# A chunked-attention and two-MLP kernel on one core: 64x64 products of scores and x put on four corners of the array instead of two

## The chip, the core and the metric

The kernel runs on one core of a Trainium2 chip. Its engines are TensorE (PE in the rows: matmuls; PEld: the loads of their weights), VectorE (DVE), ScalarE (ACT), GpSimd (POOL) and SyncE (SP), which issues the transfers between HBM and the core. Each engine works off its own list in order and waits for the others by semaphores. Matmul results go to PSUM, eight banks of 2 KB in each of 128 partitions. The metric is the device time of one execution in microseconds.

## The reference

```python
# attention in chunks of 64 tokens: 8 batches, 8 heads, 576 tokens, head dimension 64
scores = 1/8 * q_c @ k_c.T            # 64x64 for each chunk and head
attn = exp(scores - rowmax); attn = attn / (rowsum + 1e-9)
x = attn @ v_c                        # then reshaped to 4608 tokens x 512
# first MLP, 512 -> 1024 -> 512
h = x @ w_in;  sm = softmax(h);  solu = h * sm
x = (layernorm(solu) * g_ln) @ w_out
# second MLP, 512 -> 2048 -> 512
h = x @ w_in2;  g = max(h, 0) + alpha * min(h, 0)
out = g @ w_out2
```

All inputs are float32.

## The kernel before

The 4608 tokens are 36 tiles of 128. In each tile lie two chunks (c) of 64 tokens with 8 heads, and the heads are numbered by three bits (g, w, e in the code). Phase 1 does attention and the first MLP tile by tile and converts the weights of the second MLP beside it; phase 2, from about 520 us on, does the second MLP and is not touched by the change.

Each tile goes through short stages with two-letter names, and the lists FIRST and STEP write out by hand in which order they are emitted; every engine gets its own instructions in that order. FIRST covers the start. STEP then runs thirteen times, for i = 10, 12, ... 34, two tiles a round (the last has one transposed tile left); `qk+3` in it means stage qk of tile i+3. The stages that matter here:

- `qk` (L383 on): the scores, 16 products of 64x64 in float32, q against k, into a tile sc of one PSUM bank; two tiles' scores share the two banks of the pool ps_z, which the tile zt uses at other times.
- `qm` (VectorE): row maximum (nm) and difference (e), read from sc. `qe` (ScalarE): exponential. `qs`, `qn`: row sum and scaling.
- `tr` (TensorE): four 128x128 transposes of the attention into a bank et. `te` (ScalarE): its copy ets to SBUF.
- `pv` (L440 on): 16 products of 64x64, v against ets, into a bank xd. `xh` (ScalarE) and `xl` (VectorE) split xd in a high and a low part.
- `hm`: h = x @ w_in, 24 matmuls of 512 columns into the two banks of the single tile h. `hx` (VectorE, maximum), `he` (ScalarE, exponential) and `so` (VectorE, writes sl) read h; the next `hm` may write h when `so` is done with it.
- `zt`: eight transposes of the normalized sl into tile zt; `zh`, `zl` split it. `ya`, `yb`: the matmuls yps with w_out.
- `conv`: conversion of a block of the second MLP's weights, with hi, pos and neg on ScalarE.

A 64x64 product uses a quarter of the 128x128 array: the half of the rows from which its operands come (partitions 0 to 63 or 64 to 127 of SBUF) and the half of the columns that stand for its output's partitions. I call these quarters corners, (row half, column half). In `qk` and `pv` the operands' partitions and the output's are the same slice r, so that only (0,0) and (1,1) occur, one after the other:

```python
r = slice(64 * e, 64 * e + 64)
nc.tensor.matmul(ps[r, c, g, w], t[r, 0, c, g, w], t[r, 1, c, g, w], start=True, stop=True)
```

The pool ps_a holds two banks with the tags sc and et. In the STEP rounds et and xd of the odd tile use one of them and those of the even tile the other (function `bank`).

Of the kernel before, what the change touches and what calls it, by code (L numbers as in the profile page):

```python
# [45 lines left out]
def order(text):  # L46
# [3 lines left out]

FIRST_TILES = 10
FIRST = order(
    """
# [19 lines left out]
    """  # L73
    tr+1 zh-2 v+4 q+6 hm+0 zl-2 conv+0 tr+2 te+1 hx+0 qk+3 te+2 pv+1 qk+4 qm+3 he+0 qm+4 xh+1 so+0 pv+2
    xl+1 ya-5 qe+3 zt-1 qs+3 conv+0 sq+0 qe+4 qs+4 ye-6 yx-5 xh+2 hm+1 zh-1 zv+0 xl+2 v+3 pw+0 hx+1 yb-5
# [22 lines left out]
def tile_chunk_attention_solu_prelu(  # L98
# [75 lines left out]
    def phase1():  # L174
        with ExitStack() as c1, ExitStack() as c0:
# [14 lines left out]
            yp = R("y", 4)  # L190
            ps_a = L("ps_a", 1, space=PSUM)
            ps_h = L("ps_h", 1, space=PSUM)
            ps_z = R("ps_z", 1, space=PSUM)
            ps_y = R("ps_y", 2, space=PSUM)
# [181 lines left out]

            pair = [None]

            def bank(i):
                return "sc" if i >= FIRST_TILES + 2 and i % 2 == 0 else "et"  # L380

            def qk(i):
                if i < FIRST_TILES + 3:  # L383
                    ps = ps_a.tile([128, 2, 2, 2, CH], F32, name="sc", tag="sc")
                elif i % 2:
                    pair[0] = ps_z.tile([128, 2, 2, 2, 2, CH], F32, name="sc", tag="zt")
                    ps = pair[0][:, 0]
                else:
                    ps = pair[0][:, 1]
                t = qs.pop(i)  # L390
                for c in range(2):
                    for g in range(2):
                        for w in range(2):
                            for e in range(2):
                                r = slice(64 * e, 64 * e + 64)
                                nc.tensor.matmul(  # L396
                                    ps[r, c, g, w], t[r, 0, c, g, w], t[r, 1, c, g, w], start=True, stop=True
                                )
                sc[i] = ps

            def qmax(i):
                ps = sc.pop(i)
                nm = sm.tile([128, H], F32, name="nm", tag="nm", bufs=1)
                psv = ps.rearrange("q c g w k -> q (c g w) k")
                nc.vector.tensor_reduce(out=nm, in_=psv, op=ALU.max, axis=AX.X, negate=True)
                e = at.tile([128, H, CH], F32, name="e", tag="e")
                nc.vector.tensor_tensor(out=e, in0=psv, in1=nm.unsqueeze(2).to_broadcast([128, H, CH]), op=ALU.add)
                ee[i, 0] = e
# [19 lines left out]
            def tr(i):  # L428
                assert i not in rs
                e = ee.pop((i, 1)).rearrange("q (j w) k -> q j (w k)", w=2)  # L430
                ps = ps_a.tile([128, NP, 128], F32, name="et", tag=bank(i))
                for p in range(NP):
                    nc.tensor.transpose(ps[:, p], e[:, p], ident)
                att[i, 0] = ps
# [6 lines left out]
            def pv(i):  # L441
                assert ("v", i) in done
                a = att.pop((i, 1)).rearrange("k (c g e q) -> k c g e q", c=2, g=2, e=2)
                v = vs.pop(i)
                if i < 8:
                    ps = ps_y.tile([128, NP, 2, CH], F32, name="xd", tag="yps")
                else:
                    ps = ps_a.tile([128, NP, 2, CH], F32, name="xd", tag=bank(i))
                for c in range(2):
                    for g in range(2):  # L450
                        for e in range(2):
                            for w in range(2):
                                r = slice(64 * w, 64 * w + 64)
                                nc.tensor.matmul(  # L454
                                    ps[r, 2 * g + e, c], v[r, c, g, e], a[r, c, g, e], start=True, stop=True
                                )
                pvs[i] = ps.rearrange("d p c q -> d p (c q)")

            def xhigh(i):
                if 2 <= i < 6:  # L460
                    t = xt[i // 2 - 1]
                    xh, xl = t[:, i % 2, 0], t[:, i % 2, 1]
                else:
                    xh = xp.tile([128, NP, 128], F32R, name="xh", tag="xh")
                    xl = xp.tile([128, NP, 128], F32R, name="xl", tag="xl")
                nc.scalar.activation(out=xh, in_=pvs[i], func=AF.Copy)
                xs[i, 0] = xh, xl

            def xlow(i):
                xh, xl = xs[i, 1] = xs.pop((i, 0))  # L470
                nc.vector.tensor_tensor(out=xl, in0=pvs.pop(i), in1=xh.bitcast(F32), op=ALU.subtract)

# [181 lines left out]
            for name, i in FIRST:  # L654
                if name in "ho" and i >= UO:
                    run_post(next(u for u in range(len(units)) if ("a", u) not in done) + 1)
                else:
                    emit(name, i)
            twice = TWICE
            k = 0  # L660
# [533 lines left out]
```

## Time and profile before

| | |
|---|---|
| median of three runs | 1255.19 us (1254.41 to 1256.19) |
| the profiled execution, its own time | 1252.65 us |
| its span, first to last instruction | 1250.9 us |
| TensorE busy | 1222.3 us, 98% |
| VectorE, ScalarE, GpSimd busy | 72%, 54%, 26% |
| share of TensorE in the chain that ended last | 88% |

The profile is one execution. Its rows give start and length of instructions in us from the span's start, merged where equal ones follow each other (x32 is 32 of them); brackets at a row's end say how long the engine had been idle before and what ended that. Ends of matmuls are modelled and neighbours overlap in the pipeline, so TensorE's work is measured by distances between starts. PEclk is the granted clock of TensorE, 1.00 for 2.4 GHz and 0.50 for 1.2 GHz.

### The profile page before, as it was taken

The page shows a single profiled execution, that of the slowest core. Times are in us where ns is not written, and L with a number is a line of the kernel's source. Part 1 is how long each engine was busy: PE and PEld are TensorE (multiplying, and loading weights), DVE is VectorE, ACT ScalarE, POOL GpSimd, SP SyncE. Part 2 cuts the span into 40 slices and gives each one's busy share as a digit, 9 for nine tenths or more (in the row PEclk, how much of TensorE's full clock was granted, in tenths as well). Part 3 has the DMA queues.
Part 4 walks back from the last instruction along what each step waited for, and adds up shares of the span by engine and source line. Part 5 has one row for each costly group of instructions (what it writes and reads, how often), then busy time and mean ns, then how long its engine had stood idle before and what let it go on. Part 6 is the DMA issues. An engine that isn't in the chain of part 4 may idle for free.

```text
span 1250.9 us, 20791 instructions
## 1 busy us (share of the span) xinstructions
PE 1222.3 (98%) x7830; PEld 1058.4 (85%) x7830; DVE 898.9 (72%) x1274; ACT 674.7 (54%) x1061; POOL 330.0 (26%) x336
## 2 busy tenths in 40 slices
PE   5889999999999999999999999999999999999998
PEld 4778888888888888888888999988888888889998
DVE  7986676667766766337777777777885967859594
ACT  6684555555655555345666666566543434444442
POOL 3454266445755765323020030300000000000000
PEclk8899999999999999999999999999999999999999
DMA  9534276555755652559653545479983837547463
GB/s 355 185 85 127 84 223 200 159 171 170 236 172 185 207 189 104 188 222 361 225 185 122 169 156 180 148 255 305 334 336 124 297 101 245 176 142 244 140 215 101
DMA packets 148277, 244.64 MB, mean 196 GB/s; under 512 B 14672, under 2 KB 81360, under 8 KB 147664
## 3 DMA queue, kind: packets, MB, share of 16 engines
q1 hardware_dynamic: 145872, 241.22, 56.7%
q10 hardware_dynamic: 2304, 2.10, 0.5%
q8 instruction: 61, 1.00, 0.3%
q14 instruction: 40, 0.33, 0.1%
HBM read 154.93 MB, written 88.34 MB: 194 GB/s over the span
## 4 chain that ended last, share of the span: by engine, by line
PE 88%; DVE 2%; issue 1%; ACT 1%; DVEq 0%
PE h L480 9%; PE ov L1032 8%; PE ox L1032 8%; PE oz L1032 8%; PE hv L789 7%; PE hx L789 7%; PE hz L789 7%; PE yps L170 5%; PE yps L172 5%; PE yps L171 5%; PE h L486 5%; PE oy L1032 4%; PE hy L789 3%; PE zt L546 2%; PE xd L454 2%; PE sc L396 2%
## 5 line engine op out<-in xcount | busy, mean ns | idle before, releaser
L828 DVE SCALAR_TENSOR_TENSOR g<-ng,nal,g 128x512 f32<-128x512 f32 (+1 forms) x160 | 119.6, 747 | 51.2 <-ACT g L701 49.4
L701 ACT ACTIVATE ng<-g 128x512 f32<-128x512 f32 (+1 forms) x120 | 70.8, 590 | 121.9 <-DVE g L695 121.3
L170 PE MATMUL yps<-zz,wo_h 128*128 128x512 f32 x288 | 115.3, 400 | 0.0
L172 PE MATMUL yps<-zz,wo_l 128*128 128x512 f32 x288 | 112.6, 391 | 0.0
L171 PE MATMUL yps<-zz,wo_h 128*128 128x512 f32 x288 | 112.3, 390 | 0.0
L789 PE MATMUL hv<-th,w 128*128 128x512 f32 (+1 forms) x320 | 105.1, 369 | 0.4 <-DVE g L695 0.3
L789 PE MATMUL hz<-th,w 128*128 128x512 f32 (+1 forms) x320 | 104.9, 368 | 0.4 <-DVE g L695 0.2
L789 PE MATMUL hx<-th,w 128*128 128x512 f32 (+1 forms) x320 | 104.7, 368 | 0.2 <-ACT g L701 0.2
L494 DVE TENSOR_REDUCE st<-h 128x1 f32<-128x1024 f32 x36 | 44.1, 1224 | 69.2 <-PE h L486 69.2
L1032 PE MATMUL ov<-rhi,w 128*128 128x512 f32 (+3 forms) x308 | 93.1, 364 | 0.0
L1032 PE MATMUL ox<-rhi,w 128*128 128x512 f32 (+1 forms) x304 | 92.8, 366 | 0.0
L1032 PE MATMUL oz<-rhi,w 128*128 128x512 f32 (+1 forms) x304 | 92.8, 366 | 0.0
L701 ACT ACTIVATE rhi<-rt 128x1024 fp32r<-128x1024 f32 (+1 forms) x56 | 54.1, 970 | 63.2 <-PE ov L1032 18.0
L698 POOL TENSOR_TENSOR yt<-y,y 128x512 f32<-128x512 f32 (+1 forms) x20 | 26.2, 1333 | 219.7 <-DMA y<-yd 219.7
L500 ACT ACTIVATE eh<-h,st 128x1024 f32<-128x1024 f32 x36 | 40.2, 1115 | 70.0 <-DVE st L494 66.8
L698 DVE TENSOR_TENSOR rlo<-rt,rhi 128x1024 fp32r<-128x1024 f32 (+1 forms) x56 | 61.5, 1105 | 15.3 <-ACT rhi L701 14.9
L701 ACT ACTIVATE g<-g 128x512 f32<-128x512 f32 (+1 forms) x120 | 70.4, 586 | 2.6
L480 PE MATMUL h<-wi_h,xh 128*128 128x512 f32 x256 | 71.4, 401 | 0.0
L480 PE MATMUL h<-wi_l,xh 128*128 128x512 f32 x256 | 68.6, 390 | 0.0
L789 PEld LDWEIGHTS hv<-th,w 128*128 128x128 f32 x320 | 59.6, 188 | 9.4 <-DVE g L695 0.9
L789 PEld LDWEIGHTS hz<-th,w 128*128 128x128 f32 x320 | 59.6, 188 | 8.6 <-DVE g L695 1.2
L789 PEld LDWEIGHTS hx<-th,w 128*128 128x128 f32 x320 | 59.6, 188 | 8.1 <-ACT g L701 0.6
(175 smaller groups left out, 3198.2 us busy)
## 6 DMA issues: line engine op xcount, KB each, us to landing
gd<-g SPq DMA_DIRECT2D x96, 256.0 KB, 2.9
qkt<-in_qk SPq DMA_DIRECT2D x36, 512.0 KB, 5.0
w<-wod SPq DMA_DIRECT2D x28, 448.0 KB, 5.0
gd<-g SPq DMA_DIRECT2D x64, 192.0 KB, 1.8
raw<-in_moe_w_out SPq DMA_DIRECT2D x24, 511.8 KB, 4.3
rc<-gd SPq DMA_DIRECT2D x22, 512.0 KB, 4.0
rd<-gd SPq DMA_DIRECT2D x22, 512.0 KB, 4.9
vt<-in_v SPq DMA_DIRECT2D x36, 256.0 KB, 4.3
```

The lines of the kernel that those rows point to most:

```text
L170: nc.tensor.matmul(o, lh, rh, start=first, stop=False)
L171: nc.tensor.matmul(o, lh, rl, start=False, stop=False)
L172: nc.tensor.matmul(o, ll, rh, start=False, stop=last)
L480: nc.tensor.matmul(ps[:, n], xh[:, kk], w[:, kk, 512 * n:512 * n + 512], start=(kk == 0 and w is wi_h), stop=False,)
L486: nc.tensor.matmul(ps[:, n], xl[:, kk], wi_h[:, kk, 512 * n:512 * n + 512], start=False, stop=(kk == K1 - 1),)
L494: nc.vector.tensor_reduce(out=st[:, 0:1], in_=hs[i], op=ALU.max, axis=AX.X, negate=True)
L500: nc.scalar.activation(out=e, in_=hs[i], func=AF.Exp, bias=st[:, 0:1], accum_out=st[:, 1:2])
L698: eng.tensor_tensor(out=out, in0=a, in1=b, op=ALU.subtract)
L701: nc.scalar.activation(out=out, in_=in_, func=func, **k)
L789: nc.tensor.matmul(self.ps[x], w[:, a, i, k], d[:, k], start=(p not in CHAINED and k + j == 0), stop=(k == 1 and j == 2), skip_group_check ...
L828: nc.vector.scalar_tensor_tensor(out=self.g[t], in0=self.n[t], scalar=nal_sb[:, f:f + 1], in1=self.g[t], op0=ALU.mult, op1=ALU.add)
L1032: nc.tensor.matmul(bank[key, m][:, e:f], W[2 * j + k][:, a, i, 128 * m:128 * m + 128], d[:, k, e:f], start=(p not in CHAINED and j + k + q ...
```

## The change

From tile 13 on (QUAD), `qk` and `pv` go through all four corners in the order (0,0), (1,1), (0,1), (1,0), four products at a time. The outputs of products with operands in rows 0 to 63 go to one PSUM bank and those of rows 64 to 127 to another, so each of a tile's sc and xd lies across two banks, and two tiles share them half and half. For scores these are the banks of ps_z as before. For et and xd, the two banks of ps_a are given back after FIRST, and a pool ps_b with one two-bank tile (tag ax) takes their place: a pair of tiles has its two et in it, then its two xd. For this the axes of v in HBM are laid out otherwise from tile 13 on. In STEP, `te+1` moves up to follow `tr+1`, `qk+4` moves ahead of `pv+1`, and `pv+2` moves up behind `pv+1`. The readers' access patterns follow the new places; what they compute stays. Tiles 0 to 12 of `qk` and `pv` are done as before.

```diff
--- before.py
+++ after.py
@@ -49,6 +49,8 @@
 FIRST_TILES = 10
+QUAD = FIRST_TILES + 3
+CORNERS = ((0, 0), (1, 1), (0, 1), (1, 0))
...
@@ -71,7 +73,7 @@
 STEP = order(
-    tr+1 zh-2 v+4 q+6 hm+0 zl-2 conv+0 tr+2 te+1 hx+0 qk+3 te+2 pv+1 qk+4 qm+3 he+0 qm+4 xh+1 so+0 pv+2
+    tr+1 zh-2 te+1 v+4 q+6 hm+0 zl-2 conv+0 tr+2 hx+0 qk+3 te+2 qk+4 pv+1 pv+2 qm+3 he+0 qm+4 xh+1 so+0
...
@@ -188,8 +190,10 @@
             ztp = R("zt", 1)
             wop = R("wo1", 1)
             yp = R("y", 4)
-            ps_a = L("ps_a", 1, space=PSUM)
             ps_h = L("ps_h", 1, space=PSUM)
+            ca = c0.enter_context(ExitStack())
+            ps_a = ca.enter_context(tc.tile_pool(name="ps_a", bufs=1, side="left", space=PSUM))
+            ps_b = []
             ps_z = R("ps_z", 1, space=PSUM)
             ps_y = R("ps_y", 2, space=PSUM)
 
@@ -374,37 +378,51 @@
                 nc.gpsimd.memset(ex[:, :, CH:CH + 1], 1e-9)
             ss, zz_, pvs, rs = {}, {}, {}, {}
 
-            pair = [None]
-
-            def bank(i):
-                return "sc" if i >= FIRST_TILES + 2 and i % 2 == 0 else "et"
+            pair = {}
+
+            def half(key, i, shape, name):
+                if i % 2:
+                    pair[key] = ps_b[0].tile([128, 2, *shape], F32, name=name, tag="ax")
+                return pair[key]
 
             def qk(i):
-                if i < FIRST_TILES + 3:
+                t = qs.pop(i)
+                if i < QUAD:
                     ps = ps_a.tile([128, 2, 2, 2, CH], F32, name="sc", tag="sc")
-                elif i % 2:
-                    pair[0] = ps_z.tile([128, 2, 2, 2, 2, CH], F32, name="sc", tag="zt")
-                    ps = pair[0][:, 0]
-                else:
-                    ps = pair[0][:, 1]
-                t = qs.pop(i)
-                for c in range(2):
+                    for c in range(2):
+                        for g in range(2):
+                            for w in range(2):
+                                for e in range(2):
+                                    r = slice(64 * e, 64 * e + 64)
+                                    nc.tensor.matmul(
+                                        ps[r, c, g, w], t[r, 0, c, g, w], t[r, 1, c, g, w], start=True, stop=True
+                                    )
+                    sc[i] = ps.rearrange("q (x c) g w k -> q x (c g w) k", x=1)
+                    return
+                if i % 2:
+                    pair["sc"] = ps_z.tile([128, 2, 2, 2, 2, CH], F32, name="sc", tag="zt")
+                ps = pair["sc"][:, :, 1 - i % 2]
+                for w in range(2):
                     for g in range(2):
-                        for w in range(2):
-                            for e in range(2):
-                                r = slice(64 * e, 64 * e + 64)
-                                nc.tensor.matmul(
-                                    ps[r, c, g, w], t[r, 0, c, g, w], t[r, 1, c, g, w], start=True, stop=True
-                                )
-                sc[i] = ps
+                        for e, c in CORNERS:
+                            r = slice(64 * e, 64 * e + 64)
+                            nc.tensor.matmul(
+                                ps[64 * c:64 * c + 64, e, w, g], t[r, 0, c, g, w], t[r, 1, c, g, w],
+                                start=True, stop=True,
+                            )
+                sc[i] = ps.rearrange("q e w g k -> q e (w g) k")
 
             def qmax(i):
                 ps = sc.pop(i)
                 nm = sm.tile([128, H], F32, name="nm", tag="nm", bufs=1)
-                psv = ps.rearrange("q c g w k -> q (c g w) k")
-                nc.vector.tensor_reduce(out=nm, in_=psv, op=ALU.max, axis=AX.X, negate=True)
+                x, j = ps.shape[1:3]
+                nmv = nm.rearrange("q (x j) -> q x j", x=x)
+                nc.vector.tensor_reduce(out=nmv, in_=ps, op=ALU.max, axis=AX.X, negate=True)
                 e = at.tile([128, H, CH], F32, name="e", tag="e")
-                nc.vector.tensor_tensor(out=e, in0=psv, in1=nm.unsqueeze(2).to_broadcast([128, H, CH]), op=ALU.add)
+                nc.vector.tensor_tensor(
+                    out=e.rearrange("q (x j) k -> q x j k", x=x), in0=ps,
+                    in1=nmv.unsqueeze(3).to_broadcast([128, x, j, CH]), op=ALU.add,
+                )
                 ee[i, 0] = e
 
             def qexp(i):
@@ -428,7 +446,10 @@
             def tr(i):
                 assert i not in rs
                 e = ee.pop((i, 1)).rearrange("q (j w) k -> q j (w k)", w=2)
-                ps = ps_a.tile([128, NP, 128], F32, name="et", tag=bank(i))
+                if i <= FIRST_TILES:
+                    ps = ps_a.tile([128, NP, 128], F32, name="et", tag="et")
+                else:
+                    ps = half("et", i, [NP, 128], "et")[:, 1 - i % 2]
                 for p in range(NP):
                     nc.tensor.transpose(ps[:, p], e[:, p], ident)
                 att[i, 0] = ps
@@ -440,12 +461,27 @@
 
             def pv(i):
                 assert ("v", i) in done
-                a = att.pop((i, 1)).rearrange("k (c g e q) -> k c g e q", c=2, g=2, e=2)
                 v = vs.pop(i)
+                a = att.pop((i, 1))
+                if i >= QUAD:
+                    a = a.rearrange("k (e w c q) -> k e w c q", e=2, w=2, c=2)
+                    ps = half("xd", i, [2, 2, 2, CH], "xd")[:, :, 1 - i % 2]
+                    for c in range(2):
+                        for e in range(2):
+                            for g, w in CORNERS:
+                                r = slice(64 * g, 64 * g + 64)
+                                nc.tensor.matmul(
+                                    ps[64 * w:64 * w + 64, g, e, c], v[r, c, e, w], a[r, e, w, c], start=True, stop=True
+                                )
+                    pvs[i] = ps.rearrange("d g e c q -> d g e (c q)")
+                    return
+                a = a.rearrange("k (c g e q) -> k c g e q", c=2, g=2, e=2)
                 if i < 8:
                     ps = ps_y.tile([128, NP, 2, CH], F32, name="xd", tag="yps")
+                elif i <= FIRST_TILES:
+                    ps = ps_a.tile([128, NP, 2, CH], F32, name="xd", tag="et")
                 else:
-                    ps = ps_a.tile([128, NP, 2, CH], F32, name="xd", tag=bank(i))
+                    ps = half("xd", i, [NP, 2, CH], "xd")[:, 1 - i % 2]
                 for c in range(2):
                     for g in range(2):
                         for e in range(2):
@@ -454,7 +490,7 @@
                                 nc.tensor.matmul(
                                     ps[r, 2 * g + e, c], v[r, c, g, e], a[r, c, g, e], start=True, stop=True
                                 )
-                pvs[i] = ps.rearrange("d p c q -> d p (c q)")
+                pvs[i] = ps.rearrange("d (g e) c q -> d g e (c q)", g=2)
 
             def xhigh(i):
                 if 2 <= i < 6:
@@ -463,11 +499,12 @@
                 else:
                     xh = xp.tile([128, NP, 128], F32R, name="xh", tag="xh")
                     xl = xp.tile([128, NP, 128], F32R, name="xl", tag="xl")
-                nc.scalar.activation(out=xh, in_=pvs[i], func=AF.Copy)
+                nc.scalar.activation(out=xh.rearrange("d (g e) t -> d g e t", g=2), in_=pvs[i], func=AF.Copy)
                 xs[i, 0] = xh, xl
 
             def xlow(i):
                 xh, xl = xs[i, 1] = xs.pop((i, 0))
+                xl, xh = (t.rearrange("d (g e) t -> d g e t", g=2) for t in (xl, xh))
                 nc.vector.tensor_tensor(out=xl, in0=pvs.pop(i), in1=xh.bitcast(F32), op=ALU.subtract)
 
             def hmm(i):
@@ -656,6 +693,8 @@
                     run_post(next(u for u in range(len(units)) if ("a", u) not in done) + 1)
                 else:
                     emit(name, i)
+            ca.close()
+            ps_b.append(c0.enter_context(tc.tile_pool(name="ps_b", bufs=1, side="left", space=PSUM, reuse_waits="tile")))
             twice = TWICE
             k = 0
             while ("p", k) in done:
@@ -1175,7 +1214,9 @@
-        "in_v": np.ascontiguousarray(heads(inputs["v"], (0, 4, 5, 1, 2, 3, 6))),
+        "in_v": np.concatenate([
+            heads(inputs["v"], (0, 4, 5, 1, 2, 3, 6))[:QUAD], heads(inputs["v"], (0, 2, 5, 1, 3, 4, 6))[QUAD:],
+        ]),
```

On TensorE, in the step for i = 28 and behind the h matmuls: before, with the waits that each row has (et: transposes, sc: scores, xd: attention by v).

```order
L433 MATMUL et<-ident,e 128x128 [waits DVE_49]
L433 MATMUL et<-ident,e 128x128 x3
L396 MATMUL sc<-qkt 64x64 [waits DMAHW5_49,DVE_49]
L396 MATMUL sc<-qkt 64x64 x15
L454 MATMUL xd<-ets,vt 64x64 [waits Activation_49]
L454 MATMUL xd<-ets,vt 64x64 x15
L396 MATMUL sc<-qkt 64x64 [waits DMAHW7_49]
L396 MATMUL sc<-qkt 64x64 x15
L454 MATMUL xd<-ets,vt 64x64 [waits Activation_49]
L454 MATMUL xd<-ets,vt 64x64 x15
L170 MATMUL yps<-zz,wo_h 128x512
```

The same place on TensorE in the changed kernel.

```order
L454 MATMUL et<-ident,e 128x128 [waits DVE_49,Activation_49]
L454 MATMUL et<-ident,e 128x128 x3
L409 MATMUL sc<-qkt 64x64 [waits DMAHW5_49,DVE_49]
L409 MATMUL sc<-qkt 64x64 x15
L409 MATMUL sc<-qkt 64x64 [waits DMAHW7_49]
L409 MATMUL sc<-qkt 64x64 x15
L473 MATMUL xd<-ets,vt 64x64 [waits Activation_49]
L473 MATMUL xd<-ets,vt 64x64 x31
L172 MATMUL yps<-zz,wo_h 128x512
```

Both groups of sc now stand ahead of both of xd, the second transpose has a wait for ScalarE more, and the second xd has none left.

On ScalarE, in a step with a weight conversion: before (zz: the high part of zt; ets: the copies of the two et; eh: the exponential of h; xh: the high part of x).

```order
L560 ACTIVATE zz<-zt 128x2x4x128 [waits PE_49]
L236 ACTIVATE hi<-f_3303 128x512 [waits DMAHW1_49,Pool_49]
L236 ACTIVATE hi<-s_3296 128x512 [waits DMAHW3_49]
L148 ACTIVATE pos<-raw,b_63 128x512 [waits DMAHW7_49]
L149 ACTIVATE neg<-raw,b_63 128x512
L438 ACTIVATE ets<-et 128x512 [waits PE_49] x2
L500 ACTIVATE eh,st<-h,st 128x1024 [waits DVE_49,Pool_49]
L466 ACTIVATE xh<-xd 128x512 [waits PE_49]
```

The same place on ScalarE in the changed kernel.

```order
L597 ACTIVATE zz<-zt 128x2x4x128 [waits PE_49]
L459 ACTIVATE ets<-et 128x512 [waits PE_49]
L240 ACTIVATE hi<-f_3297 128x512 [waits DMAHW1_49,Pool_49]
L240 ACTIVATE hi<-s_3290 128x512 [waits DMAHW3_49]
L150 ACTIVATE pos<-raw,b_63 128x512 [waits DMAHW7_49]
L151 ACTIVATE neg<-raw,b_63 128x512
L459 ACTIVATE ets<-et 128x512 [waits PE_49]
L537 ACTIVATE eh,st<-h,st 128x1024 [waits DVE_49,Pool_49]
L502 ACTIVATE xh<-xd 128x512 [waits PE_49]
```

The first copy ets now stands ahead of hi, pos and neg. The order of instructions on VectorE, GpSimd and SyncE is the same in both kernels.

## Rows read from the trace of the kernel before

**Rows 1.** The page: busy time by engine; the chain that ended last, by engine.
```profile
PE 1222.3 (98%) x7830; PEld 1058.4 (85%) x7830; DVE 898.9 (72%) x1274; ACT 674.7 (54%) x1061; POOL 330.0 (26%) x336
...
PE 88%; DVE 2%; issue 1%; ACT 1%; DVEq 0%
```

**Rows 2.** Busy us in stretches: PE, PEld, DVE, ACT, POOL, PEclk, DMA share, GB/s.
```profile
250.00:300.00 50.00, 50.00 (x423) 42.42 (x420) 34.49 (x58) 26.74 (x45) 23.72 (x25) 1.00 0.56 176
...
400.00:450.00 50.00, 50.00 (x367) 41.96 (x366) 35.33 (x56) 28.55 (x48) 34.69 (x37) 1.00 0.63 216
```

**Rows 3.** Groups by shape, count | busy us, mean ns | idle before: the 64x64 products.
```profile
L396 PE MATMUL sc<-qkt 64*64 64x64 f32 x1152 | 44.8, 233 | 14.9 <-DMA qkt<-in_qk 4.9 <-issue 3.3 <-DVE r L419 3.2
L454 PE MATMUL xd<-ets,vt 64*64 64x64 f32 x1152 | 43.1, 230 | 0.0
```

**Rows 4.** Timeline of TensorE in one step: start us, length us, instruction, count.
```profile
420.17 0.60 PE L433 MATMUL et<-ident,e 128*128 128x128 f32 x4
420.70 1.15 PE L396 MATMUL sc<-qkt 64*64 64x64 f32 x32
421.68 1.10 PE L454 MATMUL xd<-ets,vt 64*64 64x64 f32 x32
422.62 1.10 PE L396 MATMUL sc<-qkt 64*64 64x64 f32 x32
423.55 1.10 PE L454 MATMUL xd<-ets,vt 64*64 64x64 f32 x32
424.58 0.50 PE L170 MATMUL yps<-zz,wo_h 128*128 128x512 f32 x1
...
427.46 1.04 PE L546 MATMUL zt<-ident,sl 128*128 128x128 f32 x8
428.36 1.16 PE L480 MATMUL h<-wi_h,xh 128*128 128x512 f32 x4
```

**Rows 5.** L396 alone, from one group's start: PE and PEld with counts, PEclk, DMA.
```profile
420.69:420.79 0.10, 0.09 (x2) 0.09 (x4) 1.00 1.22 287
420.69:420.84 0.15, 0.14 (x4) 0.14 (x6) 1.00 1.37 300
420.69:420.89 0.20, 0.19 (x6) 0.19 (x8) 1.00 1.13 266
420.69:420.95 0.26, 0.25 (x8) 0.25 (x10) 1.00 1.07 283
```

**Rows 6.** L454 alone, the same at half clock; then that stretch's timeline.
```profile
29.30:29.50 0.20, 0.10 (x2) 0.10 (x4) 0.50 0.91 369
29.30:29.60 0.30, 0.20 (x4) 0.20 (x6) 0.50 1.08 437
29.30:29.70 0.40, 0.30 (x6) 0.30 (x8) 0.50 0.94 379
29.30:29.82 0.52, 0.42 (x8) 0.42 (x10) 0.50 1.04 386
...
29.40 1.98 PE L454 MATMUL xd<-ets,vt 64*64 64x64 f32 x32
31.16 1.92 PE L396 MATMUL sc<-qkt 64*64 64x64 f32 x32
```

**Rows 7.** Timeline of VectorE in the step of rows 4.
```profile
420.37 1.23 DVE L494 TENSOR_REDUCE st<-h 128x1 f32<-128x1024 f32 x1 [1.15 <-PE h L486]
423.76 0.69 DVE L405 TENSOR_REDUCE nm<-sc 128x8 f32<-128x512 f32 x1 [2.17 <-PE sc L396]
...
426.93 1.28 DVE L510 SCALAR_TENSOR_TENSOR sl<-h,st,eh 128x1024 f32<-128x1024 f32 x1
428.13 0.08 DVE L510 DVE_READ_ACCUMULATOR sl<-h,st,eh 128x1 f32 x1
428.13 0.69 DVE L471 TENSOR_TENSOR xl<-xd,xh 128x512 fp32r<-128x512 f32 x1
```

**Rows 8.** Timeline of ScalarE in the step of rows 4.
```profile
414.46 1.03 ACT L560 ACTIVATE zz<-zt 128x1024 fp32r<-128x1024 f32 x1 [1.25 <-PE yps L172]
...
417.71 0.59 ACT L438 ACTIVATE ets<-et 128x512 f32<-128x512 f32 x1
420.81 0.60 ACT L438 ACTIVATE ets<-et 128x512 f32<-128x512 f32 x1 [2.51 <-PE et L433]
...
422.83 0.60 ACT L466 ACTIVATE xh<-xd 128x512 fp32r<-128x512 f32 x1
```

**Rows 9.** Timelines of TensorE and VectorE where zt and h meet in other steps.
```profile
169.08 1.04 PE L546 MATMUL zt<-ident,sl 128*128 128x128 f32 x8
170.01 0.47 PE L480 MATMUL h<-wi_h,xh 128*128 128x512 f32 x1
...
456.17 1.04 PE L546 MATMUL zt<-ident,sl 128*128 128x128 f32 x8
457.09 0.47 PE L480 MATMUL h<-wi_h,xh 128*128 128x512 f32 x1
...
482.99 0.08 DVE L510 DVE_READ_ACCUMULATOR sl<-h,st,eh 128x1 f32 x1
...
484.68 1.04 PE L546 MATMUL zt<-ident,sl 128*128 128x128 f32 x8
485.47 0.71 PE L480 MATMUL h<-wi_h,xh 128*128 128x512 f32 x2
```

**Rows 10.** Who waited for whom: total us, times, longest.
```profile
DVE nm L405 <- PE sc L396: 31.5, 16, 6.9
...
PE h L480 <- DVE sl L510: 3.0, 3, 1.4
```

## The prediction

> **What bounds the kernel now.** I read the page's totals first: TensorE is busy 98% of a span of 1250.9 us and makes 88% of the chain that ended last; VectorE is at 72%, ScalarE at 54% [rows 1]. The changed code runs in the thirteen rounds of the STEP table (twelve of them with two tiles, called steps here), in the second half of phase 1, so the windows there come next: in each 50 us TensorE is busy all 50 at a granted clock of 1.00, VectorE some 35, ScalarE 27 to 29 [rows 2]. So the price of the change is what it does to TensorE's own time, unless a new wait opens a hole.
>
> The third view is the timeline of TensorE in one step [rows 4]. It is to be read by the distance between starts, since ends of matmuls are modelled. The four groups of 64x64 products (sc, xd, sc, xd) start at 420.70, 421.68, 422.62 and 423.55, and the next work at 424.58. A group is 16 products, each two instructions in the trace: 576 products are written for sc, and 1152 are recorded [rows 3]. A group in the run of groups takes 0.93 to 0.94 us, so 29.2 ns an instruction and 58.4 ns a product.
>
> **What the corners cost now.** Before, a product at corner (0,0) alternates with one at (1,1). The question is what the next product waits for: its corner, or its turn. The start of a group tells, where no corner holds a product. The counted instructions of the group [rows 5] are 2 matmuls in the first 0.10 us, 4 after 0.15, 6 after 0.20, 8 after 0.26. So the second product, whose corner has been free since the 128-wide transposes, starts some 55 ns after the first; the third, which comes back to the first corner, another 55 to 60 later. First use of a corner and reuse have the same distance.
>
> The same group at half the clock [rows 6]: 2, 4, 6, 8 matmuls after 0.2, 0.3, 0.4 and 0.52 us, and 1.76 us a group (29.40 to 31.16), 110 ns a product; there too the second product waits for its turn at a free corner. The distance doubles with the clock, so it is time of the array, about 128 of its cycles for a product of 64 columns in two halves (128/2.4 is 53 ns, 128/1.2 is 107). The reading that fits both: a product's second half waits for its first half, which is at the same corner, and matmuls start in program order, so the next product can start only together with that second half. Two corners are then enough to keep that pace, and two more stay unused however they are ordered.
>
> A rule of the Trainium skill stands on this side: "TensorE: Matmul & The Clock Gate", Part 3 (what overlaps and what doesn't), says that matmuls start and end strictly in program order, with no reordering. By it the pace term is 0, as taken here; another page says the opposite for corners, in the first rival.
>
> **The change part by part.**
> 1. Four corners in turn: 23 groups of sc (tiles 13 to 35) and 23 of xd, 46 groups of 16, so 736 products. In the program each product's two halves stay neighbours. No row shows a pace on four corners. Bound above by reuse mattering a little: the windows cannot tell 55 from 58 ns, so at most 3 ns of 736 products, 2.2 us gained. Bound below, in this reading: nothing. I take 0, the reading of rows 5 and 6, and keep 2.2 for the range.
> 2. The order sc, sc, xd, xd in place of sc, xd, sc, xd. TensorE's groups are the same four, and passing from sc to xd costs nothing now, 0.93 to 0.98 us like a plain group [rows 4]. But VectorE waits for the second sc: it has finished the row maximum of h at 421.60 (420.37 + 1.23), stands idle 2.17 us, and starts nm at 423.76, some 0.2 us after the last matmul of the second sc [rows 7]. In sum this wait is 31.5 us [rows 10]. In the new order the second sc ends where the first xd ended, 0.93 us earlier, and so does what follows on VectorE in line: two nm, two e, two small ones, and sl at 426.93, over at 428.21.
> 3. That line has someone waiting. sl is the last reader of the h tile, and the next h group on TensorE may write it only then. The transposes zt start at 427.46 and h at 428.36, 0.90 us later and 0.15 behind the end of sl [rows 4, 7]. Where sl has been over for long (483.07) the same pair is 0.79 apart: 484.68 and 485.47 [rows 9]. The first and the last of the eleven tight steps have 0.93 (169.08, 170.01) and 0.92 (456.17, 457.09) [rows 9]; others 0.90. So 0.11 to 0.14 us a step go to this wait, 11 x 0.12 = 1.3 us. The page's list shows only 3.0 us in 3 times for it [rows 10], since small holes are left out; so I go by the starts. With sl 0.93 us earlier the hole closes, and sl has 0.8 us to spare. Gain: 1.3 us.
> 4. New waits by the two-bank tile. The second transpose of a step now waits for ScalarE's copy of the first (ets). That copy moves up in ScalarE's order, ahead of the weight conversion (hi, pos, neg). It stood at 417.71 behind them; the zz before them ends at 415.49, so it now ends near 416.1 and the transpose at 420.17 is 4 us away [rows 4, 8]. Queued behind the copy are the conversions, 0.6 us later than now, in front of a ScalarE idle of 2.51 us. The first xd now needs both copies. The second one ends at 421.41, and the first xd moves from 421.68 to 422.62: 1.2 us to spare. A satisfied second wait costs TensorE nothing visible (sc to xd above has two). Should it cost what a binding wait costs in item 3, it would be 12 x 0.11 = 1.3 us; I take 0 and keep 1.3. Were the cover gone, each us that a copy is late would cost 12 us.
> 5. The copy xh may now start only after xd in place of between: at about 424.6 instead of 422.83, done at 425.2, and the h group that reads it starts past 428. The second xh also waits for VectorE's xl of the first, which has moved up with the rest. No one else waits. Reads across two banks: nm, e, xh, xl take 0.6 to 0.7 us a piece [rows 7, 8]. If each VectorE read took 0.1 more, it would eat 0.4 of the 0.8 us in item 3.
> 6. v is laid out otherwise in HBM, with the same tile shape, the same number of loads and the same place in SP's order; nothing is added to a queue.
> What is late next, once the hole of item 3 is closed: TensorE itself.
>
> **Sum.** Against the profiled run's 1252.65 us (span 1250.9): 0 for the pace, -1.3 for the hole, 0 for the waits, so 1251.35. The median of the three runs is 2.54 us above that run: 1255.19 - 1.3 = 1253.9 us. Ends of the unknown costs: -2.2 (item 1) and +1.3 (item 4), with +1.3 more if the hole stays because reads of two banks are slow; the runs themselves spread over 1.8 us.
>
> **Rivals.** *Four corners run at twice the pace.* If a corner were what the next product waits for, with halves of different products free to pass each other, a product would take 29 ns: 736 x 29.2 = 21.5 us less. VectorE's line would then start nm at about 421.8 (420.70 + 2 x 0.47 + 0.2) and end sl 4.45 later, near 426.3, while h is ready near 426.4 (427.46 - 4 x 0.47 + 0.79), so the hole of item 3 would nearly close as well: 1255.2 - 21.5 - 0.6 = 1233 us. "TensorEngine Tiling (Array Packing)", Tiling Modes (Key Properties), of the Trainium skill says that tiles work independently and that different tiles load weights and multiply in parallel, with four of them in the 64x64 mode; by it the pace halves. The trace speaks against: at a group's start the second corner is free and waits all the same [rows 5, 6]. It speaks for it that the present two corners share a bank, and the new ones don't.
> *Neighbours in the same columns can't overlap: slower.* Today neighbours share neither rows nor columns of the array. In the new order two of four neighbours, (1,1) to (0,1) and (1,0) to (0,0), share their columns. If a product there can't start along with the second half of the one before, it comes up to 58 ns later: 8 such pairs x 46 groups = 368, x 58.3 = 21.5 us, so 1253.9 + 21.5 = 1275.4. It decides from about 10 ns a pair on (368 x 0.010 = 3.8 us, against the 1.3 gained). For it: no row shows such neighbours. Against it: they differ in rows and in bank.
> *The order alone turns into a hole:* item 4's cover would have to fail by over 1.2 us; the copies' times are too regular for more than a small part of the slower chance.
>
> **Chances.** The forecast 0.80, four corners faster 0.14, slower neighbours 0.06. A measurement of this kernel tells about 0.2% (2.5 us) from no change. Within the forecast's case, 0.09 lie over 2.5 us below (part of item 1's bound with item 3), 0.70 within, 0.01 above. So faster 0.23, same 0.70, slower 0.07. Range: 1253.9 - 2.2 - 0.7 for the spread of runs gives 1251.0; 1253.9 + 2.6 + 1.0 gives 1257.5. The rivals stay outside, 0.20 together.
>
> **What would show it.** Right: in a step the starts of sc, sc, xd, xd still lie 0.93 us apart; zt to h shrinks to 0.79; nm starts 0.93 us earlier in the step; TensorE stays at 50 of 50 in the windows. Wrong: group distances near 0.47 (first rival) or over 1.0 (second); a hole ahead of the second transpose or of the first xd that ends with ets; or a zt to h that stays at 0.90, which would mean that something other than sl held h.

## The result, and the profile after

The changed kernel takes 1233.66 us (median of four runs, 1232.14 to 1235.99) beside 1254.8 us for the kernel before on the same chip: a ratio of 0.984, 95% interval 0.9825 to 0.9855, or 21.1 us less. The forecast of 1253.9 and its range (1251.0 to 1257.5) missed it; the first rival, "four corners run at twice the pace", had 1233.

The page of the changed kernel, busy time by engine and the chain that ended last, answers to [rows 1]:

```profile
PE 1202.9 (98%) x7830; PEld 1038.4 (84%) x7830; DVE 900.6 (73%) x1274; ACT 674.0 (55%) x1061; POOL 327.7 (27%) x336
...
PE 85%; DVE 3%; ACT 2%; issue 2%; DMA 0%; DVEq 0%
```

TensorE has as many instructions as before and is busy 19.4 us less. The changed kernel's windows answer to [rows 2]:

```profile
250.00:300.00 50.00, 50.00 (x433) 41.83 (x435) 35.83 (x56) 27.91 (x46) 26.34 (x27) 1.00 0.61 185
400.00:450.00 50.00, 50.00 (x477) 41.65 (x475) 38.20 (x58) 32.56 (x54) 32.91 (x36) 1.00 0.57 197
```

TensorE is still busy all 50 us at a granted clock of 1.00, so no large hole was closed there: its own work has become shorter. Where, the timeline of TensorE in the step of [rows 4] tells (ahead of it the first sc of the step before):

```profile
379.47 1.16 PE L409 MATMUL sc<-qkt 64*64 64x64 f32 x64
...
405.83 0.60 PE L454 MATMUL et<-ident,e 128*128 128x128 f32 x4
406.36 1.16 PE L409 MATMUL sc<-qkt 64*64 64x64 f32 x64
407.34 1.11 PE L473 MATMUL xd<-ets,vt 64*64 64x64 f32 x64
408.39 0.50 PE L172 MATMUL yps<-zz,wo_h 128*128 128x512 f32 x1
...
411.25 1.04 PE L583 MATMUL zt<-ident,sl 128*128 128x128 f32 x8
412.19 1.17 PE L517 MATMUL h<-wi_h,xh 128*128 128x512 f32 x4
```

Two groups of sc now take 0.98 us together, where one took that before. From the first sc to the next work (yps), a step's 64 products take 2.03 us (406.36 to 408.39) and took 3.88 [rows 4]: some 29 ns a product instead of 58. The step, from its sc to the next one's, is 406.36 - 379.47 = 26.89 us and 26.87 in most steps; in the trace of before it was 28.70 in most. The difference of some 1.83 us is nearly that of four groups at 0.467 less each (16 x 29.2 ns; 1.87 in all). From the first step's sc to the last zt it is 345.8 us, and 366.6 before: 20.8 of the 21.1 us. The length of a step is the best ruler for all that follows, since within a trace it repeats to 0.05 us (but for the first step, the last, and single ones), while the stretch ahead of the steps differs by up to 5 us between traces.

The hole of the prediction's item 3 is still there: zt to h is 0.94 in this step and 0.92 in nine others (it was 0.90 in [rows 4]). Counted from a group's start as in [rows 5]:

```profile
406.35:406.45 0.10, 0.09 (x4) 0.09 (x8) 1.00 0.99 266
406.35:406.50 0.15, 0.14 (x8) 0.14 (x12) 1.00 1.98 342
406.35:406.55 0.20, 0.19 (x12) 0.19 (x16) 1.00 1.85 318
406.35:406.61 0.26, 0.25 (x16) 0.25 (x20) 1.00 1.65 292
```

4, 8, 12, 16 matmuls where there were 2, 4, 6, 8. Products 1 and 2 are at corners (0,0) and (1,1) in both kernels; only from the third on does the place differ.

### The profile page after: what moved, and what is told of

The parts are those of the page before. It is cut to its first block, busy times and chain, and to the rows that moved or that the text cites. A ratio compares the mean times of both kernels' runs of the same rounds, so it can differ in the third digit from the quotient of the medians.

```text
span 1232.3 us, 20795 instructions
## 1 busy us (share of the span) xinstructions
PE 1202.9 (98%) x7830; PEld 1038.4 (84%) x7830; DVE 900.6 (73%) x1274; ACT 674.0 (55%) x1061; POOL 327.7 (27%) x336
## 4 chain that ended last, share of the span: by engine, by line
PE 85%; DVE 3%; ACT 2%; issue 2%; DMA 0%; DVEq 0%
PE h L517 9%; PE ov L1071 8%; PE ox L1071 8%; PE oz L1071 8%; PE hv L828 6%; PE hz L828 6%; PE hx L828 6%; PE yps L172 5%; PE yps L174 5%; PE yps L173 5%; PE h L523 5%; PE oy L1071 4%; PE hy L828 3%; PE zt L583 2%; DVE g L734 2%
```

## Experiments

Two readings were open at first. *Bank*: before, a product waits since its neighbour with the other row half writes the same PSUM bank. *Corners*: a corner is busy with a product for 117 ns, whatever its neighbours do, so that two corners give only half the pace of four.

### Which corners alternate

Four kernels go through the corners by parts (the list PARTS; which corners are in a part differs from kernel to kernel), with the row halves' banks as in the changed kernel. The edit, cut, in `qk` (in `pv` alike):

```diff
-                for w in range(2):
-                    for g in range(2):
-                        for e, c in CORNERS:
+                for part in PARTS:
+                    for w in range(2):
+                        for g in range(2):
+                            for e, c in part:
```

> The changed kernel, but each group of 16 products goes through two corners at a time: (0,0) and (1,1) alternate for 8 products, then (0,1) and (1,0) for 8. The row halves keep a PSUM bank each. Theory "bank" (in the kernel before, a product waits because its neighbour with the other row half writes the same bank): the pace stays at 29 ns a product, groups 0.47 us apart, 1233.7 us as in the changed kernel, within 2. Theory "corners" (two corners are too few, four are needed): 58 ns a product, groups 0.93 us apart, 736 x 29.2 ns = 21.5 us more, 1255 us, less up to 1.3 if the new order alone closes the hole between zt and h.

> The changed kernel, but the pairs that alternate share their row half: (0,0) with (0,1) for 8 products, then (1,1) with (1,0). They write the same bank in different partitions. Theory "bank" in its narrow form (only row halves that share a bank wait): 29 ns a product, 1233.7 us. Bank in its wide form (any two products in one bank wait) or a shared entry of the rows: 58 ns, 1255 us. Theory "corners": 58 ns, 1255 us.

> The changed kernel, but the pairs that alternate share their column half: (0,0) with (1,0) for 8 products, then (0,1) with (1,1). They write the same partitions in different banks. Theory "bank": 29 ns a product, 1233.7 us. The rival of the prediction that neighbours in the same columns can't overlap: 58 ns, 1255 us. Theory "corners": 58 ns, 1255 us.

> The changed kernel, but four products in a row at each corner before the next one, row halves in banks of their own. By both theories a corner must be busy with a product for some time; the group shows how long. Theory "bank": with two corners in turn giving 29 ns, a corner would be free again after at most 58 ns, so about 58 ns a product, groups about 0.93 us apart, 1255 us (more if the reload of weights then shows). Theory "corners": with two corners at 58 ns, a corner alone gives 58 to 117 ns, groups 0.93 to 1.87 us apart, 1255 to 1298 us.

Measured: two_corners 1238.71 us, ratio to before 0.9881 (0.9863 to 0.9899); row_neighbours 1238.66 and col_neighbours 1240.63 in one run each; one_corner 1267.21 in one run. The step is 27.40 us in all three kernels with pairs, whatever the two corners share, and 29.65 with one corner at a time. So neither shared rows nor shared columns nor the bank makes a difference; the number of corners does. But the pairs lie between both theories' numbers: from the first sc to yps the 64 products take 2.67 us, which is 0.64 more than in the changed kernel, so some 39 ns a product where 29 or 58 was expected. The counts from a group's start, for two_corners:

```profile
410.34:410.44 0.10, 0.09 (x2) 0.09 (x4) 1.00 0.93 307
410.34:410.49 0.15, 0.14 (x4) 0.14 (x6) 1.00 1.46 355
410.34:410.60 0.26, 0.25 (x8) 0.25 (x10) 1.00 1.61 347
410.34:410.63 0.29, 0.28 (x8) 0.28 (x10) 1.00 1.57 339
410.34:410.66 0.32, 0.31 (x12) 0.31 (x14) 1.00 1.50 320
410.34:410.80 0.46, 0.45 (x18) 0.45 (x22) 1.00 1.19 285
410.34:411.00 0.66, 0.65 (x30) 0.65 (x34) 1.00 1.12 292
```

and for one_corner:

```profile
430.86:430.96 0.10, 0.09 (x1) 0.09 (x2) 1.00 0.58 205
430.86:431.01 0.15, 0.14 (x2) 0.14 (x3) 1.00 2.39 396
430.86:431.06 0.20, 0.19 (x3) 0.19 (x4) 1.00 2.07 359
430.86:431.12 0.26, 0.25 (x4) 0.25 (x5) 1.00 1.74 307
430.86:431.14 0.28, 0.27 (x4) 0.27 (x5) 1.00 1.61 285
430.86:431.17 0.31, 0.30 (x6) 0.30 (x7) 1.00 1.52 271
```

With one corner, behind the first matmul, single ones start some 58 ns apart: the two halves of a product take their turns at their corner. With two corners there are two in each 58 ns, exactly as in [rows 5], although the banks are apart here: *bank* is out as the reason for the old pace. What starts together in [rows 5] is therefore not the two halves of one product but one half each of two products at two corners. Shorter windows on the same group of the kernel before say it too:

```profile
420.69:420.72 0.03, 0.02 (x2) 0.02 (x2) 1.00 0.33 136
420.69:420.79 0.10, 0.09 (x2) 0.09 (x4) 1.00 1.22 287
420.69:420.81 0.12, 0.11 (x3) 0.11 (x4) 1.00 1.35 307
```

Two matmuls start at once and the third only 0.1 us later, where one_corner has a single matmul in its first 0.10 us. After 0.28 us the pace of two_corners and one_corner rises: by then the next corners have begun, while the first still have products left (a part is 8 products in two_corners, 4 in one_corner). For one_corner that is when the first corner has started 5 of its 8 instructions, for two_corners 5 of 8 at each. The rows do not name the corner of a matmul; this is counted from the 58 ns that a corner takes for each. So the list goes on to another corner while up to three instructions wait at the one before. And corners do not wait for each other's order; the timeline of two_corners, where sc ends and xd begins:

```profile
410.35 1.39 PE L410 MATMUL sc<-qkt 64*64 64x64 f32 x58
411.52 0.27 PE L475 MATMUL xd<-ets,vt 64*64 64x64 f32 x2
411.57 0.28 PE L410 MATMUL sc<-qkt 64*64 64x64 f32 x3
...
413.02 0.50 PE L172 MATMUL yps<-zz,wo_h 128*128 128x512 f32 x1
```

All 64 of sc stand ahead of xd in the program, and xd's first two start before the last six of sc. So the theory that replaced *corners* is *a queue for each corner*: one instruction in 58 ns at each, independent of the others.

### Two products in a row

This theory was put to a number ahead of the next run.

```diff
-                    for g in range(2):
-                        for e, c in CORNERS:
+                    for e, c in CORNERS:
+                        for g in range(2):
```

> The changed kernel, four corners in turn, but two products in a row at each. Theory "a queue for each corner": a corner works off its own instructions at one in 58 ns, and the common list moves on while a corner has two of them waiting. Then the corners start one after the other and all four are soon busy: about 0.24 us more for the first two groups than in the changed kernel, as much again for the next two at most, 12 x 0.24 to 12 x 0.48, so 1236.6 to 1239.5 us, and starts at up to four corners overlapping out of the program's order. Theory "in order" (an instruction starts only when the one ahead of it in the list has started): the second product at a corner holds all behind it, 117 ns for two products, 58 ns a product, groups 0.93 us apart, 1255 us.

Measured: 1233.95 us in one run, steps of 27.00, so 0.13 more than in the changed kernel. The pace of the changed kernel is all but kept, and *in order* is out. The expectation was too high, since it let only two instructions wait at a corner. Four of them in a row already cost nothing at a group's start:

```profile
405.50:405.60 0.10, 0.09 (x4) 0.09 (x7) 1.00 1.15 348
405.50:405.65 0.15, 0.14 (x7) 0.14 (x11) 1.00 1.57 328
```

Four matmuls in the first 0.10 us, at 58 ns each per corner, are four corners: the list has gone past four instructions at the first one, of which one has started and three wait. That agrees with the two kernels above.

### The order and the corners apart

order_alone keeps the changed kernel's order and pools, and takes the old corners, one bank for a tile's sc and xd each, and the old v:

```diff
-                ps = pair["sc"][:, :, 1 - i % 2]
+                ps = pair["sc"][:, 1 - i % 2]
...
-                        for e, c in CORNERS:
+                        for w in range(2):
+                            for e in range(2):
...
-                if i >= QUAD:
+                if i >= 99:
```

> The changed kernel with the old products: corners (0,0) and (1,1) only, a tile's sc and xd in one bank each, v laid out as before; the new order in STEP and the two-bank tile for et and xd stay. Items 2 to 4 of the prediction: the pace stays 58 ns a product (groups 0.93 us apart), nm starts 0.93 us earlier in the step, zt to h shrinks from 0.90 to 0.79, no hole ahead of the second transpose or the first xd, and the time falls by 1.3 us against the kernel before (ratio 0.999). Rival: the distance from zt to h has another cause and stays 0.90, ratio 1.000. Rival: the wait for both copies or the two-bank tile costs TensorE, up to 0.11 us a step, ratio up to 1.001.

> The kernel of order_alone a second time, for a second trace. There the step had shrunk from 28.70 to 28.59 us, but the stretch ahead of the steps was 2.9 us longer than in the trace of before and the one behind them 1.4 us. If those two come by chance from run to run, the second trace has them within 1 us of before, and a time near 1253; if the new pools or the order make them, they come again, and the time is near 1255.

Measured: 1254.88 us (11 runs), ratio 1.0007 (0.9997 to 1.0018); the second time 1253.7 in one run. In the steps, item 3 holds as forecast. The timeline of TensorE in order_alone:

```profile
251.02 2.08 PE L410 MATMUL sc<-qkt 64*64 64x64 f32 x64
252.94 2.03 PE L490 MATMUL xd<-ets,vt 64*64 64x64 f32 x64
257.78 1.04 PE L583 MATMUL zt<-ident,sl 128*128 128x128 f32 x8
258.57 1.17 PE L517 MATMUL h<-wi_h,xh 128*128 128x512 f32 x4
```

zt to h is 0.79, in every step; two groups take 1.92; and nm starts 2.13 us after the first sc where it was 3.06 [rows 4, 7], so 0.93 earlier. A step is 28.59 us, 0.11 less, as worked out. But one step, that of tile 26, is 0.75 longer than the others in both traces of this kernel, with this wait of TensorE in it (the row is of the second trace):

```profile
411.13 1.06 PE L583 MATMUL zt<-ident,sl 128*128 128x128 f32 x8 [0.53 <-DVE st L542]
```

VectorE's scaling of sl ahead of that zt took 1.65 us there, and 1.22 in the same step before; why was not tested. So the steps and what follows up to the last zt come to 0.57 us less than before in both traces, not 1.3. The time doesn't show even that: its interval starts at 0.9997, and 0.57 us less would be 0.9995. The 2.9 us ahead of the steps in the first trace were 0.8 in the second, the 1.4 behind them 0.2. Most of that therefore comes and goes, as in the changed kernel, whose own two traces differ by 3.0 us ahead of the steps; whether a few tenths of it belong to this kernel is not shown.

corners_alone is the opposite, the changed kernel with the order of before:

```diff
-    tr+1 zh-2 te+1 v+4 q+6 hm+0 zl-2 conv+0 tr+2 hx+0 qk+3 te+2 qk+4 pv+1 pv+2 qm+3 he+0 qm+4 xh+1 so+0
+    tr+1 zh-2 v+4 q+6 hm+0 zl-2 conv+0 tr+2 te+1 hx+0 qk+3 te+2 pv+1 qk+4 qm+3 he+0 qm+4 xh+1 so+0 pv+2
```

> The changed kernel with the old order in STEP (sc, xd, sc, xd), four corners and two banks as in the changed kernel. If the order matters at the new pace: the first xd must wait for both copies ets, which end 0.7 us behind the second transpose, while one group of sc now covers only 0.47, so a hole of some 0.24 us a step, 12 x 0.24 = 2.9 us; and the second sc, with nm and sl behind it, comes 0.47 later, which the h group waits for, up to 11 x 0.47 = 5.2 us. So 1236.6 to 1241.8 us against 1233.7. Rival, the order is worth nothing beside the corners: 1233.7 within 1.

Measured: 1250.7 us, ratio 0.9975 (0.9962 to 0.9987). Of the 21 us only some 4 are left: more was lost than either expectation said. The timeline of TensorE (with one row of ScalarE) and its waits in corners_alone:

```profile
384.65 0.60 PE L454 MATMUL et<-ident,e 128*128 128x128 f32 x4
...
391.09 0.69 PE L409 MATMUL sc<-qkt 64*64 64x64 f32 x32
392.34 0.69 PE L473 MATMUL xd<-ets,vt 64*64 64x64 f32 x32 [0.55 <-ACT ets L459]
392.85 0.65 PE L409 MATMUL sc<-qkt 64*64 64x64 f32 x32
393.92 0.69 PE L473 MATMUL xd<-ets,vt 64*64 64x64 f32 x32 [0.42 <-ACT xh L502]
...
391.20 1.09 ACT L459 ACTIVATE ets<-et 128x512 f32<-128x512 f32 x2 [5.93 <-PE et L454]
```

```profile
PE xd L473 <- ACT ets L459: 6.1, 11, 0.6
PE xd L473 <- ACT xh L502: 5.1, 11, 0.9
```

The step is 28.20 us, 1.33 more than in the changed kernel: from the first sc to the first xd 1.25 us instead of 0.49 (half of the 0.98 for two groups), from the second sc to the second xd 1.07. The first hole was expected, but at 0.24 us, not 0.55. The expectation had only the second copy ets run behind the second transposes, but both do: the first, whose transposes ran at 384.65, waits until 391.20, behind the second ones, since both et now lie in one tile and `te+1` stands behind `tr+2` in the list. The second hole was not expected: since both tiles' xd share both banks, the copy xh of the first must be over before the second may be written. Two xd in a row do away with that, two sc in a row cover the second copy, and `te+1` ahead of `tr+2` lets the first one run early; what each of these three moves is worth by itself was not run. So the new order is worth next to nothing at the old pace, and some 17 of the 21 us (1250.7 - 1233.7) with the four corners and their two-bank layout.

### The hole between zt and h

so_early moves sl ahead of the second row maximum:

```diff
-qk+4 pv+1 pv+2 qm+3 he+0 qm+4 xh+1 so+0
+qk+4 pv+1 pv+2 qm+3 he+0 so+0 qm+4 xh+1
```

> The changed kernel with the stage so (it writes sl, the last read of h) ahead of the second row maximum of scores on VectorE. If sl is what holds the h group behind zt in the changed kernel too (0.94 us from zt to h, sl over 0.14 before h), sl is over 1.5 us earlier, zt to h shrinks to 0.79, and 11 x 0.14 = 1.6 us are gained: 1232.1 against 1233.7. Rival, something else holds h: no change. Rival, the second row maximum, now 1.4 us later, makes the next step's transposes wait: slower.

Measured: 1240.58 us, ratio 0.9899 (0.9886 to 0.9913), 7 us slower than the changed kernel, with steps of 27.60. zt to h does shrink to 0.82; as zt itself comes later here, that alone doesn't show that sl holds h (the next kernel does). The tile zt lies in the banks of sc, and its transposes now wait until VectorE has read sc (e):

```profile
390.99 1.06 PE L583 MATMUL zt<-ident,sl 128*128 128x128 f32 x8 [0.65 <-DVE e L422]
```

small_on_gpsimd shortens the line on VectorE instead, and small_but_one does so with `i % 2 or i == 22` as its condition:

```diff
-                nc.vector.tensor_scalar(
+                (nc.vector if i % 2 else nc.gpsimd).tensor_scalar(
```

> The changed kernel with one of the two small VectorE operations ahead of sl (the sum plus 1e-9, times 1024) on GpSimd for the even tiles; GpSimd is idle from 407.5 to 410.3 in the step, and its input is there at 408.5. If VectorE's unbroken line from nm to sl is what sets the end of sl, sl ends 0.17 us earlier in the step, the wait of h for sl (0.13 us in most steps) closes, the step shrinks from 26.87 to about 26.74, and some 10 x 0.13 = 1.3 us are gained: 1232.4 against 1233.7, ratio to the kernel before 0.983. Rival: VectorE must then wait for GpSimd, or another reader of h is late, and the step stays at 26.87 or grows.

> As small_on_gpsimd, but tile 22 keeps the small operation on VectorE: in its step GpSimd was busy until 330.7 and did it 1.3 us late, and that step was 28.12 us long instead of 26.87. Expected: steps of 26.77 throughout, 10 x 0.10 = 1.0 us less than changed_again of the same call. Rival: the 2.9 us by which small_on_gpsimd was over the changed kernel have another cause than that one step (1.35), and it stays slower.

> The changed kernel once more, on the same chip as small_but_one: 1233.7 us within 1, ratio 0.984, steps of 26.87.

Measured: 1236.51 us, ratio 0.9859 (0.9841 to 0.9877); 1234.82, ratio 0.984 (0.9826 to 0.9855); and the changed kernel 1233.89, ratio 0.9838 (0.9818 to 0.9857). The steps shrink to 26.78 and 26.76, but for one of 28.12 in the first, where GpSimd was busy and did the operation late, and which the second mends (26.91). That late step also shows what holds h:

```profile
330.57 1.04 PE L583 MATMUL zt<-ident,sl 128*128 128x128 f32 x8
332.73 1.16 PE L517 MATMUL h<-wi_h,xh 128*128 128x512 f32 x4 [1.12 <-DVE sl L547]
...
332.49 0.08 DVE L547 DVE_READ_ACCUMULATOR sl<-h,st,eh 128x1 f32 x1
```

h starts some 0.15 us behind the end of sl (332.57), as it does in the steps of [rows 4, 7], although zt to h is 2.16 here and 0.90 there. So sl is what holds h. From the first step's sc to the last zt small_but_one takes 345.2 us, the changed kernel 345.8 and, the second time, 346.05: the gain of 0.6 to 0.9 us is there in the steps and not to be told in the time. The late step is 1.35 of the 2.9 us by which small_on_gpsimd lies over the changed kernel; the rest stays open, and the intervals of the two ratios overlap. No kernel here beats the changed one measurably.

## Why the prediction was wrong

- **Item 1 failed, and with it the forecast.** The step was the reading of [rows 5, 6]: "a product's second half waits for its first half, which is at the same corner, and matmuls start in program order". The first half of the sentence is right (one_corner). The second is not: at another corner the list's next instructions start at once (two_corners, two_in_a_row). The prediction took the first two matmuls of [rows 5] for the two halves of one product; they are first halves of two, at (0,0) and (1,1). The pace alone fits both readings: two corners that work at 117 ns a product, or one product after the other at 58; half the clock doubling it [rows 6] fits both as well. But the prediction's two statements don't fit each other: if a second half waits for its first, the two matmuls that start at once (420.69:420.72) can't be one product, and its "second product ... some 55 ns after the first" isn't in the trace, where the third matmul comes 0.1 us after the first. Shorter windows would have told this before any run. No row of before had one corner alone or more than two, so the pace on four stayed open even then, and the bound of 2.2 us was made within the reading instead of from outside it. "TensorE: Matmul & The Clock Gate", Part 3, of the Trainium skill, which the prediction leaned on, says matmuls start strictly in program order; the rows of two_corners above disagree, with xd starting ahead of the last six of sc.
- **The first rival was right** in mechanism (halves of different products pass each other) and nearly in size: 736 x 29.2 = 21.5 us less, measured 20.8 from the first step to the last zt. "TensorEngine Tiling (Array Packing)", Tiling Modes (Key Properties), of the Trainium skill says that tiles work independently; at 29.2 ns a product on four corners, 58.4 on two, the traces agree. What the prediction held against it, a free second corner that waits, was a misreading, as said above. What it held in its favour, the banks, made no difference on two corners (two_corners); four corners were not run with one bank.
- **Item 3** was right in mechanism (order_alone, small_on_gpsimd), 0.11 us a step where 0.12 was forecast, and hidden twice: at the old pace one step gives 0.75 back, and in the changed kernel the hole is still open. There sl starts 1.83 us earlier, counted from sc, but zt comes 1.87 earlier as well in the step shown (4.89 us from sc to zt, 6.76 before). The rival's 0.6 us for it were therefore not gained.
- **Item 2**: nm 0.93 us earlier, as order_alone shows. **Items 4 and 5**: no hole ahead of the second transpose or the first xd in the changed kernel, so 0 was right for the waits; that the order was what kept them at 0 the prediction said only in part (the copies, not xh). **Item 6** was not run by itself.
- **The slower rival** (neighbours in the same columns) fell: col_neighbours and row_neighbours have the same steps as two_corners to 0.01 us (the first step apart).
- **Chances**: 0.14 for the first rival was too little, as what spoke against it was a reading that shorter windows of the same trace refute. That the rival's 1233 meets the measured 1233.66 so closely is in part luck: its 0.6 us for the hole was not gained.

## What to carry to other kernels

A row that fits two mechanisms is no evidence for either: before pricing a pace at nothing, ask which row would look different under the rival, and if there is none, let the rival's time into the range. In this kernel small matmuls did best spread over all corners in short turns, one or two float32 products in a row at each; when outputs of different row halves must then go to banks of their own, group writes and reads so that no tile's reader comes between two writers of its banks. Measure a repeated step by its period in the trace, which shows 0.1 us where the total's scatter hides one or two.

## What the runs showed of the hardware

- A corner of the array takes one 64x64 float32 matmul instruction in 58 ns at a granted clock of 1.00, and a product is two: 117 ns at one corner, 58 on two, 29 on four. For pairs it makes no difference which two corners they are or whether they write one bank or two (steps of 27.40 us in all three); the four were run with a bank for each row half only.
- Corners start independently and out of the program's order, with up to three instructions waiting at one before the list stops: in two_corners xd began ahead of the last six matmuls of sc. "In order", as the first section has it for every engine, does not hold between the corners of TensorE.
- Two corners in one bank, in different partitions, run as fast as in two banks (2, 4, 8 matmuls after 0.10, 0.15, 0.26 us in both). Two row halves in one bank and the same partitions were not tried.
